# Attention and a gated two-layer network on one core: the first layer of the last four units by a Strassen scheme

## The chip, the cores and the metric

One Trainium2 chip, one of its cores. The metric is the device time of one execution in microseconds. An execution is taken several times; the median is given. A core has five engines that run side by side, each through its own list of instructions in order: PE (matrix products), DVE, ACT and POOL (elementwise work) and SP (which here only issues transfers). Semaphores tie them together.

## The reference

Attention over 4 batches, 8 heads, 768 positions and 64 dimensions, in which a query sees the keys less than 16 positions away and 24 summaries of 32 keys each; its output, 3072 tokens of 512 values, goes through a layer of 2048, a gate and a layer of 512.

```python
k_sum = k.reshape(B, H, nb, block, D).max(axis=3)
v_sum = v.reshape(B, H, nb, block, D).mean(axis=3)
scores_l = scale * np.matmul(q, k.transpose(0, 1, 3, 2))
mask_l = np.abs(pos[:, None] - pos[None, :]) < window
scores_s = scale * np.einsum('bhsd,bhnd->bhsn', q, k_sum) + np.log(block)
...
return np.matmul(a, v_all)
...
h = x @ w_in
g = np.where(h >= 1, h, np.where(h <= -1, 0.0, (h + 1) ** 2 / 4.0))
return (g @ w_out).astype(np.float32)
```

## The kernel before

The tokens are worked off in eight units of 384 (half a batch). A unit has an attention part, for four pairs of heads, and a feed-forward part. Matrix operands of the feed-forward part are split into a high half and a rest (`hi`, `lo`), and each product is the sum of three: rest by high, high by rest, high by high.

*First layer* (`ff1`, step F): for each of 16 slices f of 128 hidden values and each of four slices k of 128 inputs, three matmuls with 128 x 128 weights held in the array and 384 tokens streamed; one PSUM bank for each f, two in turn (`ps_h`). *Gate* (G, H, I, J, O): ACT takes a shifted half from PSUM and squares it, DVE takes the minimum with the value in PSUM, ACT copies the high half, POOL subtracts for the rest. *Second layer* (`ff2`, step B): for each f and each of three groups of 128 tokens, three matmuls of 512 columns into one of three PSUM banks (`ps_acc`), which collect over all f and are copied out (U) and stored (o) at the unit's end.

*Attention* (for units 2 to 7): scores for two pairs of heads at once (s), masks and maxima on DVE (n, i), exponentials on ACT (g), reciprocals on DVE (h), multiplication on POOL (l), 32 x 32 transposes on DVE (t), values on PE (p), and the split of the result into `xhi` (X, ACT) and `xlo` (L, DVE). Sums over 32 keys or values are made once for each batch (R, u, z), and copied into place by POOL (C, x).

Weights come as 64-bit numbers, and in the opening they are converted to 32 bits on ACT and DVE (a, b, c) and split by d and e; after that they stay on the chip. All transfers are issued by SP. Three texts give the order of all steps by hand, each step a letter and its indices: `OPENING`, `SECOND` and `LATER`; the last is run for each unit from 2 on. Each engine's list is the order in which the steps issue to it. PSUM has eight banks: two for F and one score block, three for `ps_acc`, three for attention.

Of the kernel before, what the change touches and what calls it, by code (L numbers as in the profile page):

```python
# [55 lines left out]
P110 H0b S13 A11 dd H0c B0a ec M130 I0b ed q21 I0c F0d0 D120 k20 ae F0d1 F0e0 F0e1 J0c F0e2 v12 F0d2 M131 J0b f130 be0
r21 f131 ce0 N120 O0c be1 E130 ce2 O0b af D130 F0d3 X11 N121 R20 ce1 F0e3 ce3 B0b L11 E131 G0d H0d I0d B0c bf1 de ee
cf1 bf0 G0e H0e T120 I0e cf0 F0f0 cf3 J0d O0d W13 F0f1 cf2 D131 F0f2 J0e df F0f3 T121 q20 G0f F110 H0f F111 W12 P121
N130 P120 N131 T130 A12 X12 I0f T131 P131 L12 F100 J0f P130 B0d O0e R21 ef O0f A13 X13 F112 L13 C20 F101 F102 F113
F103 B0e G11 G10 H10 H11 I10 B0f J10 I11 C21 F120 J11 O10 U00 F121 F122 U01 O11 F123 U02 o02 o01 o00  # L60
# [529 lines left out]
```

## Time and profile before

| | |
|---|---|
| median of 3 runs | 632.76 us (631.87 to 633.6) |
| the profiled execution | 632.96 us, of which its span is 631.2 us |
| PE busy, 272 to 344 us | 72.00 of 72.00 us |
| matmuls | 4388 on PE, as many weight loads |
| moved by DMA | 63.6 MB, all of the kernel's own by the queue of SP |

The page of the profile gives for each engine the time in which an instruction was in it. Matmuls overlap in the array, so their busy times (339 ns for one of 384 columns) are longer than the distance from one start to the next; the prediction therefore reads starts. The page divides the span into 40 slices, and shows the granted clock of the array as full from the 50th microsecond to the end.

```profile
PE   8689999999999999999999999999999999999997
DVE  5879787377836549376643737469363726411111
PEclk9879999999999999999999999999999999999999
```

### The profile page before, as it was taken

Reading aid. Unit: us, or ns where it says so; the run is one execution under the profiler, and the core shown is the slowest. Engines: PE = TensorE matmul, PEld = TensorE weight load, DVE = VectorE, ACT = ScalarE, POOL = GpSimd, SP = SyncE. Lnnn points to the kernel's source line nnn. Section 1 sums busy time; section 2 is a strip of 40 time slices with the busy share of each in tenths; the row PEclk is TensorE's granted clock in tenths of the full one; section 3 lists DMA queues with packets and bytes.
Section 4 is the critical chain, followed back from the end, with each engine's and each line's share of the span. In section 5 each row is a group of like instructions: output and inputs, shape, how many; then the busy total and the mean of one; then the engine's idle time right before and its main releaser. Section 6 shows DMA issues by size and latency. Waiting matters only on the chain.

```text
span 631.2 us, 11762 instructions
## 1 busy us (share of the span) xinstructions
PE 617.1 (98%) x4388; PEld 550.4 (87%) x4388; DVE 357.8 (57%) x822; ACT 336.7 (53%) x877; POOL 259.4 (41%) x272
## 2 busy tenths in 40 slices
PE   8689999999999999999999999999999999999997
PEld 7578888898988989898898989889898988999995
DVE  5879787377836549376643737469363726411111
ACT  2679998454547353463635436373543636343342
POOL 2578999533533333333423434333332333212221
PEclk9879999999999999999999999999999999999999
DMA  8999953181124150251213033162202210010001
GB/s 305 299 309 359 275 178 80 54 247 46 52 64 123 51 158 4 78 182 38 74 38 99 25 103 109 38 196 65 73 1 82 79 38 2 1 50 1 2 0 51
DMA packets 49770, 63.57 MB, mean 101 GB/s; under 512 B 24881, under 2 KB 33329, under 8 KB 49713
## 3 DMA queue, kind: packets, MB, share of 16 engines
q1 hardware_dynamic: 49712, 62.81, 33.5%
q8 instruction: 35, 0.57, 0.4%
q14 instruction: 23, 0.18, 0.1%
HBM read 56.51 MB, written 6.29 MB: 99 GB/s over the span
## 4 chain that ended last, share of the span: by engine, by line
PE 91%; DMA 4%; POOL 2%; DVE 1%; ACT 1%; SPq 0%; issue 0%; POOLq 0%; ACTq 0%
PE acc L464 42%; PE h L426 41%; PE o_ps L415 3%; PE s_ps L360 3%; DMA raw<-in_w_in 2%; DMA raw<-in_w_out 1%; POOL halves L175 1%; PE o_ps L332 1%; PE t_ps L320 1%; DMA first<-in_kT 1%; PE h_idle L434 0%; PE s_ps L286 0%; DVE w L163 0%; POOL e L315 0%; DVE c L158 0%
## 5 line engine op out<-in xcount | busy, mean ns | idle before, releaser
L426 PE MATMUL h<-xhi,halves 128*128 128x384 f32 x1024 | 284.7, 339 | 2.8 <-POOL halves L175 1.8
L464 PE MATMUL acc<-halves,ghi 128*128 128x512 f32 x768 | 240.4, 394 | 0.0
L455 POOL TENSOR_TENSOR glo<-t,ghi 128x384 fp32r<-128x384 f32 x128 | 129.7, 1015 | 263.7 <-ACT ghi L450 186.8
L426 PEld LDWEIGHTS h<-xhi,halves 128*128 128x128 f32 x1024 | 187.3, 188 | 9.4 <-POOL halves L175 2.7
L445 DVE SCALAR_TENSOR_TENSOR t<-h,t 128x384 f32<-128x384 f32 x128 | 70.7, 556 | 205.1 <-ACT t L442 200.4
L426 PE MATMUL h<-xlo,halves 128*128 128x384 f32 x512 | 172.0, 336 | 0.0
L464 PEld LDWEIGHTS acc<-halves,ghi 128*128 128x128 f32 x768 | 144.1, 188 | 27.8
L464 PE MATMUL acc<-halves,glo 128*128 128x512 f32 x384 | 152.4, 397 | 0.0
L439 ACT ACTIVATE t<-h,ones_half 128x384 f32<-128x384 f32 x128 | 74.0, 579 | 131.9 <-PE h L426 122.6
L405 DVE STREAM_TRANSPOSE turned_blocks<-e 32x192 f32<-32x192 f32 x288 | 106.5, 370 | 20.5 <-POOL e L393 16.4
L450 ACT CAST ghi<-t 128x384 fp32r<-128x384 f32 x128 | 65.2, 511 | 96.5 <-DVE t L445 94.8
L426 PEld LDWEIGHTS h<-xlo,halves 128*128 128x128 f32 x512 | 96.3, 188 | 4.9
L464 PEld LDWEIGHTS acc<-halves,glo 128*128 128x128 f32 x384 | 72.1, 188 | 14.5 <-issue 2.1
L381 ACT ACTIVATE e<-e,den 128x120 f32<-128x120 f32 x144 | 55.2, 386 | 26.5 <-DVE den L375 26.5
L442 ACT ACTIVATE t<-t 128x384 f32<-128x384 f32 x128 | 66.6, 522 | 2.9
L393 POOL TENSOR_TENSOR e<-e,den 128x720 f32<-128x720 f32 x24 | 33.4, 1391 | 51.0 <-DVE den L387 23.7
L175 POOL TENSOR_TENSOR halves<-w,halves 128x1024 fp32r<-128x1024 f32 x16 | 38.6, 2412 | 5.4 <-DMA q<-in_q 4.2
L381 ACT ACTIVATION_READ_ACCUMULATOR e<-e,den 128x1 f32 x144 | 27.3, 189 | 0.0
L158 DVE SCALAR_TENSOR_TENSOR c<-raw,c 128x512 int32<-128x512 int32 x32 | 22.0, 690 | 6.3 <-ACT raw L144 3.0
L368 DVE SCALAR_TENSOR_TENSOR e<-s_ps,mask_sb 128x360 f32<-128x360 f32 x48 | 22.4, 523 | 5.6 <-PE s_ps L360 5.6
L304 ACT ACTIVATE e<-e,den 128x120 f32<-128x120 f32 x48 | 18.3, 384 | 10.2 <-DVE den L299 10.2
L150 ACT ACTIVATE c<-raw 128x512 int32<-128x512 uint32 x32 | 19.8, 627 | 5.8 <-DMA raw<-in_w_in 4.8
(77 smaller groups left out, 422.3 us busy)
## 6 DMA issues: line engine op xcount, KB each, us to landing
k<-in_kwin SPq DMA_DIRECT2D x28, 360.0 KB, 4.4
v<-in_vwin SPq DMA_DIRECT2D x30, 288.0 KB, 3.4
raw<-in_w_in SPq DMA_DIRECT2D x16, 512.0 KB, 10.1
raw<-in_w_out SPq DMA_DIRECT2D x16, 512.0 KB, 10.1
out<-o SPq DMA_DIRECT2D x24, 256.0 KB, 2.3
q<-in_q SPq DMA_DIRECT2D x56, 96.0 KB, 4.0
kraw<-in_kT SPq DMA_DIRECT2D x13, 384.0 KB, 4.2
vraw<-in_vT SPq DMA_DIRECT2D x13, 384.0 KB, 5.3
```

Of the source, the lines that this page charges most:

```text
L175: nc.gpsimd.tensor_tensor(out=lo, in0=converting[i].bitcast(F32), in1=hi.bitcast(F32), op=ALU.subtract)
L368: nc.vector.scalar_tensor_tensor(out=es[c, h][:, b, j], in0=s_pss[c, p, j][:, :NT * KA].rearrange("p (t n) -> p t n", n=KA), scalar=1.0 / ...
L381: nc.scalar.activation(out=e, in_=e, func=AF.Exp, bias=dens[c, p][:, 0, j, t:t + 1], scale=1.0, accum_out=dens[c, p][:, 1, j, t:t + 1])
L393: nc.gpsimd.tensor_tensor(out=e, in0=e, in1=den.unsqueeze(2).broadcast_to([P, 2 * NT, KA]), op=ALU.mult)
L405: nc.vector.transpose(out=pt[kb * SB:(kb + 1) * SB, :, qb * SB:(qb + 1) * SB], in_=e[qb * SB:(qb + 1) * SB, :, at:at + SB])
L426: nc.tensor.matmul(hs[c, f][:, :T], weight["win", f][w][:, k * P:(k + 1) * P], x, start=(k == 0 and n == 0), stop=(k == NK - 1 and n == 2))
L439: nc.scalar.activation(out=ts[c, f], in_=hs[c, f][:, :T], func=AF.Relu, bias=ones_half, scale=0.5)
L442: nc.scalar.square(out=ts[c, f], in_=ts[c, f])
L445: nc.vector.scalar_tensor_tensor(out=ts[c, f], in0=hs[c, f][:, :T], scalar=1.0, in1=ts[c, f], op0=ALU.max, op1=ALU.min)
L450: nc.scalar.copy(out=hi, in_=ts[c, f])
L455: nc.gpsimd.tensor_tensor(out=lo, in0=ts[c, f], in1=hi.bitcast(F32), op=ALU.subtract)
L464: nc.tensor.matmul(acc[c][i], a[:, rows], weight["wout", f][w], start=(f == 0 and n == 0), stop=(f == NF - 1 and n == 2))
```

## The change

The tokens are divided anew: units of 384, 384, 256 and four of 512. From unit 3 on (`CLASSIC = 3`) the first layer is done two slices of hidden values at a time (a pair q, eight in all) by Strassen's scheme in Winograd's form. For a pair the layer is a product of two 2 x 2 block matrices: weights in blocks of 256 inputs by 128 hidden values, tokens in blocks of 256 inputs by 256 tokens. Instead of eight block products it takes seven (step 1, operands and weights being sums and differences of blocks), each of two slices of inputs by the same three split products, with 256 tokens streamed. DVE and one copy on ACT then add up the seven (step 9), through four running sums (`so_far`) and in place in PSUM. The gate works on halves of 256 tokens, and copies the high half and makes the rest for 512 at a time.

The seven weight operands of each pair are three of the old ones and four sums. These are made once, in units 1 and 2 (step %: additions on POOL and DVE, split on ACT and POOL), stored to DRAM by SP (&, six stores a pair, 48 in all), and read back in each of the four units (step {, four transfers a pair, 128 in all), issued by POOL, into a ring in the room of first-layer weights that are no longer needed. The token operands are made once for each unit: four differences on POOL (^), seven copies of high halves on ACT (<), seven subtractions on POOL (>), into the room of weights 0 to 6, one buffer each.

The second layer is issued for one group of 128 tokens at a time (step "(") and has four banks; two banks remain for attention, shared with three of the products. Scores and values are done for one pair of heads at a time. Conversions d and e of the opening are split into two instructions each, since each weight has a room of its own, and the opening no longer loads keys and queries of unit 2. One text `REST` gives the order of all steps after the opening. The core of the diff:

```diff
+BLOCKS = [[(0, 0, 6)], [(0, 6, 6)], [(1, 0, 4)], [(1, 4, 8)], [(2, 0, 8)], [(2, 8, 4), (3, 0, 4)], [(3, 4, 8)]]
+CLASSIC = 3
-SECOND = """
...
-LATER = """
...
+REST = """
+%000 r20 k20 %001 q20 %002 %010 %011 %003 %004 %012 R20 %013 %005 %006 C200 %014 s20 n200 n201 &40 r21 k21 i20 g200
...
     def convert_rest(i):
-        hi, lo = halves[i][:, 0], halves[i][:, 1]
-        nc.gpsimd.tensor_tensor(out=lo, in0=converting[i].bitcast(F32), in1=hi.bitcast(F32), op=ALU.subtract)
+        for part, piece in enumerate(pairs[i]):
+            hi, lo = weight[piece][:, 0], weight[piece][:, 1]
+            nc.gpsimd.tensor_tensor(out=lo, in0=converting[i][:, part].bitcast(F32), in1=hi.bitcast(F32), op=ALU.subtract)
...
+    def difference(c, n):
+        a, b = x_raw_tile(c, 0), x_raw_tile(c, 1)
+        out_, in0, in1 = ((a[:, 2], a[:, 1], a[:, 0]), (a[:, 1], b[:, 1], a[:, 1]), (b[:, 2], b[:, 1], a[:, 2]), (b[:, 0], b[:, 0], b[:, 2]))[n]
+        nc.gpsimd.tensor_tensor(out=out_, in0=in0, in1=in1, op=ALU.subtract)
+    def x_high(c, n):
+        x_ops[c, n] = wpool.tile([P, 2, 2, HALF], F32R, tag=f"win{n}", name=f"xop{c}_{n}")
+        nc.scalar.copy(out=x_ops[c, n][:, 0], in_=x_source(c, n))
+    def x_rest(c, n):
+        x = x_ops[c, n]
+        nc.gpsimd.tensor_tensor(out=x[:, 1], in0=x_source(c, n), in1=x[:, 0].bitcast(F32), op=ALU.subtract)
...
+    def load_set(c, q, n):
+        tag = 7 + 4 * (q % 2) + n
+        cols = sets[q, :, n * 4 * HALF:min(n * 4 + 4, 14) * HALF]
...
+        nc.gpsimd.dma_start(out=flat, in_=cols)
+    def product(c, q, n):
...
+        where, tag = ((ps_att, "att") if n in (1, 4, 5) else (ps_h, "h"))
+        hs[c, q, n] = where.tile([P, 512], F32, tag=tag, name=f"h{c}_{q}_{n}")
+        x = x_ops[c, n]
+        for kk in range(2):
+            for m, (wp, xp) in enumerate(((1, 0), (0, 1), (0, 0))):
+                nc.tensor.matmul(hs[c, q, n][:, :HALF], weights[:, wp, kk], x[:, xp, kk],
+                                 start=(kk == 0 and m == 0), stop=(kk == 1 and m == 2))
+    def combine(c, q, n):
...
+        if n == 0:
+            nc.scalar.copy(out=so_far[:, 0], in_=hs[c, q, 0][:, :HALF])
+            return
+        which, so, to = ((2, 0, 1), (4, 1, 2), (1, 0, None), (3, 1, 3), (3, 2, None), (5, 2, None), (6, 3, None))[n - 1]
+        of = hs[c, q, which][:, :HALF]
+        nc.vector.tensor_tensor(out=of if to is None else so_far[:, to], in0=of, in1=so_far[:, so], op=ALU.add)
+    def prepare(q, kk, n):
...
+            nc.gpsimd.tensor_tensor(out=a[:, 2 * n:2 * n + 2], in0=both[:, 0].bitcast(F32), in1=both[:, 1].bitcast(F32), op=ALU.add)
+        elif n < 6:
...
+            nc.vector.tensor_tensor(out=a[:, out_], in0=a[:, in0], in1=a[:, in1], op=op)
...
+                nc.gpsimd.tensor_tensor(out=a.bitcast(F32R), in0=a, in1=hi.bitcast(F32), op=ALU.subtract)
-        ps_acc = ctx.enter_context(tc.tile_pool(name="ps_acc", bufs=NTT, space=PSUM))
-        ps_att = ctx.enter_context(tc.tile_pool(name="ps_att", bufs=3, space=PSUM))
+        ps_acc = ctx.enter_context(tc.tile_pool(name="ps_acc", bufs=4, space=PSUM))
+        ps_att = ctx.enter_context(tc.tile_pool(name="ps_att", bufs=2, space=PSUM))
```

The order on PE, before, in the middle of unit 4: one slice of the first layer, then one of the second (h is the PSUM bank of a slice, acc that of 128 tokens; the last figures are the columns).

```order
L426 MATMUL h_5_4142<-xhi_2_3834,halves_727 128x384
L426 MATMUL h_5_4142<-xlo_2_3835,halves_727 128x384
L426 MATMUL h_5_4142<-xhi_2_3834,halves_727 128x384
L426 MATMUL h_5_4142<-xhi_3_3848,halves_727 128x384
L426 MATMUL h_5_4142<-xlo_3_3849,halves_727 128x384
L426 MATMUL h_5_4142<-xhi_3_3848,halves_727 128x384
L464 MATMUL acc_0_4030<-halves_727,glo_3_4113 128x512
L464 MATMUL acc_0_4030<-halves_727,ghi_3_4112 128x512 x2
L464 MATMUL acc_1_4031<-halves_727,glo_3_4113 128x512
L464 MATMUL acc_1_4031<-halves_727,ghi_3_4112 128x512 x2
```

The order on PE now, in the middle of a Strassen unit (h_4_0 is product 0 of pair 4; xop_0 its tokens, ring_4_0 its weights).

```order
L598 MATMUL h_4_0_5316<-xop_0_4500,ring_4_0_5221 128x256 x6
L598 MATMUL h_4_2_5336<-xop_2_4582,ring_4_1_5167 128x256 x6
L598 MATMUL h_4_3_5343<-xop_3_4609,ring_4_3_5241 128x256 x6
L598 MATMUL h_4_1_5358<-xop_1_4574,ring_4_0_5221 128x256 x6
L598 MATMUL h_4_4_5365<-xop_4_4624,ring_4_2_5257 128x256 x6
L694 MATMUL acc_1_4929<-halveswout_1073,glo_7_5331 128x512
L694 MATMUL acc_1_4929<-halveswout_1073,ghi_7_5330 128x512 x2
L694 MATMUL acc_0_4981<-halveswout_1073,glo_7_5331 128x512
L694 MATMUL acc_0_4981<-halveswout_1073,ghi_7_5330 128x512 x2
L598 MATMUL h_4_6_5381<-xop_6_4723,ring_4_2_5257 128x256 x6
```

A slice's twelve matmuls of 384 have become products of six matmuls of 256, and accumulations of single groups stand between them.

The order on POOL at a change of unit, before (from unit 4 to 5: rests of the gate glo, the copy of sums into keys, a multiplication of exponentials e).

```order
L455 TENSOR_TENSOR glo_15_4666<-t_15_4660,ghi_15_4665 128x384
L455 TENSOR_TENSOR glo_0_4728<-t_0_4710,ghi_0_4727 128x384
L393 TENSOR_TENSOR e_0_4725<-e_0_4725,den_0_4741 128x720
L455 TENSOR_TENSOR glo_1_4802<-t_1_4771,ghi_1_4801 128x384
L455 TENSOR_TENSOR glo_2_4855<-t_2_4820,ghi_2_4854 128x384
```

The order on POOL now, at the change from unit 2 to 3, the first with Strassen products (DMA ring is the issue of a load of weights; L486 is a difference of tokens, L498 the rest of an operand).

```order
L585 DMA ring_0_1_3321<-sets 128x1024
L585 DMA ring_1_0_3323<-sets 128x1024
L681 TENSOR_TENSOR glo_15_3311<-t_15_3244,ghi_15_3310 128x256
L629 TENSOR_TENSOR merged_1_3120<-merged_1_3120,x_1_1770 128x512
L681 TENSOR_TENSOR glo_14_3358<-t_14_3319,ghi_14_3357 128x256
L486 TENSOR_TENSOR xraw_0_2807<-xraw_1_3091,xraw_0_2807 128x512
L486 TENSOR_TENSOR xraw_1_3091<-xraw_1_3091,xraw_0_2807 128x512
L498 TENSOR_TENSOR xop_1_3361<-xraw_1_3091,xop_1_3361 128x512
L498 TENSOR_TENSOR xop_2_3386<-xraw_1_3091,xop_2_3386 128x512
L498 TENSOR_TENSOR xop_4_3407<-xraw_0_2807,xop_4_3407 128x512
L486 TENSOR_TENSOR xraw_1_3091<-xraw_1_3091 128x512
L498 TENSOR_TENSOR xop_6_3364<-xraw_1_3091,xop_6_3364 128x512
```

Where one subtraction a slice stood, there are now eight subtractions in a row, behind loads of weights and a split of weight sums.

The order on DVE before, in unit 4 (t is the gate's tile).

```order
L445 SCALAR_TENSOR_TENSOR t_11_4476<-h_11_4442,t_11_4476 128x384
L405 STREAM_TRANSPOSE turned_blocks<-e_1_4330 32x6x32 x10
L252 TENSOR_REDUCE sums<-vraw_0_4393 128x24
L253 TENSOR_SCALAR sums<-sums 128x24
L445 SCALAR_TENSOR_TENSOR t_12_4519<-h_12_4487,t_12_4519 128x384
```

The order on DVE now, in a Strassen unit (L611 adds a product to a running sum, or a running sum to a product in PSUM).

```order
L611 TENSOR_TENSOR sums_so_far<-h_4_2_5336,sums_so_far 128x256
L552 STREAM_TRANSPOSE turned_blocks<-e_2_5195 32x8x32 x3
L611 TENSOR_TENSOR sums_so_far<-h_4_4_5365,sums_so_far 128x256
L552 STREAM_TRANSPOSE turned_blocks<-e_2_5195 32x8x32 x4
L611 TENSOR_TENSOR sums_so_far<-h_4_3_5343,sums_so_far 128x256
L611 TENSOR_TENSOR h_4_1_5358<-h_4_1_5358,sums_so_far 128x256
L611 TENSOR_TENSOR h_4_6_5381<-h_4_6_5381,sums_so_far 128x256
L611 TENSOR_TENSOR h_4_3_5343<-h_4_3_5343,sums_so_far 128x256
L671 SCALAR_TENSOR_TENSOR t_8_5415<-h_4_1_5358,t_8_5415 128x256
L671 SCALAR_TENSOR_TENSOR t_9_5433<-h_4_3_5343,t_9_5433 128x256
```

Between two gate minima DVE now has seven additions for each pair of slices, each of which releases a product's bank or the gate on it.

More of the change, by code (lines that the diff above doesn't have):

```diff
@@ L56 @@
[L56 to L60, printed above, removed]
@@ L227, in window_keys @@
+        at = 0
+        for b, blk, n in BLOCKS[c]:
+            while n:
+                half, i = divmod(blk, NB)
+                m = min(n, NB - i)
+                nc.sync.dma_start(out=v_ts[c, p][:KW, at:at + m], in_=vwin[b, p, half, :, i:i + m])
+                at, blk, n = at + m, blk + m, n - m
     def window_keys(c, p):
@@ L230, in window_keys @@
         eng = {"v": nc.vector, "g": nc.gpsimd}[K_COPY[p]]
[L231 removed]
+        blocks = raws["k", c, p].rearrange("p (n q) -> p n q", q=QB)
         eng.memset(k_t[:, 0, :WIN], 0.0)
@@ new lines, in values_of_pair @@
+    def values_of_pair(c, p):
+        nt = WIDTH[c] // P
+        o_pss[c, p] = ps_att.tile([P, 512], F32, tag="att", name=f"o_ps{c}_{p}")
+        for blk in range(2 * nt):
+            t, i = divmod(blk, 2)
+            for j in range(2):
+                nc.tensor.matmul(o_pss[c, p][j * D:(j + 1) * D, blk * QB:(blk + 1) * QB], v_ts[c, p][:, blk, j * D:(j + 1) * D],
+                                 turned_blocks[:, j * nt + t, i * QB:(i + 1) * QB], start=True, stop=True)
+    hs, ts, gs, acc, outs, ring_of, merged = {}, {}, {}, {}, {}, {}, {}
@@ L457, in ff2 @@
     def ff2(c, f):
-        if f == 0:
-            acc[c] = [(ps if c == 0 else ps_acc).tile([P, DM], F32, tag="ps", name=f"acc{c}_{i}") for i in range(NTT)]
-        g_hi, g_lo = gs[c, f]
-        for i in range(NTT):
-            rows = slice(i * P, (i + 1) * P)
-            for n, (a, w) in enumerate(((g_lo, 0), (g_hi, 1), (g_hi, 0))):
-                nc.tensor.matmul(acc[c][i], a[:, rows], weight["wout", f][w], start=(f == 0 and n == 0),
-                                 stop=(f == NF - 1 and n == 2))
+        for i in range(WIDTH[c] // P):
+            ff2_rows(c, f, i)
@@ new lines, in ff2_rows @@
+    def ff2_rows(c, f, i):
+        if (c, i) not in acc:
+            acc[c, i] = (ps if c == 0 else ps_acc).tile([P, DM], F32, tag="ps", name=f"acc{c}_{i}")
+        g_hi, g_lo = gs[c, f]
+        rows = slice(i * P, (i + 1) * P)
+        first, last = (0, NF - 1) if c < CLASSIC else (1, NF - 2)
+        for n, (a, part) in enumerate(((g_lo, 0), (g_hi, 1), (g_hi, 0))):
+            nc.tensor.matmul(acc[c, i], a[:, rows], weight["wout", f][:, part], start=(f == first and n == 0), stop=(f == last and n == 2))
@@ L488, in fused_kernel @@
+        rows = mask.shape[1] * KA
+        for at, first, count in ((2, 0, 3),) if n == 0 else ((0, 2, 2), (5, 2, 2)):
+            both = bass.AP(mask.tensor, mask.offset + first * KA, [[QB * rows + KA, 2], [rows, QB], [1, count * KA]])
+            nc.sync.dma_start(out=mask_sb[:, at:at + count], in_=both)
     steps = {
```

488 lines of the change are left out of this document (318 added, 170 removed).

## The prediction

> **What bounds the kernel now.** I read the head of the page first, then the chain, then equal stretches of the steady part.
>
> ```profile
> span 631.2 us, 11762 instructions
> PE 617.1 (98%) x4388; PEld 550.4 (87%) x4388; DVE 357.8 (57%) x822; ACT 336.7 (53%) x877; POOL 259.4 (41%) x272
> PE 91%; DMA 4%; POOL 2%; DVE 1%; ACT 1%; SPq 0%; issue 0%; POOLq 0%; ACTq 0%
> core 0: us, PE busy (x) PEld busy (x) DVE busy (x) ACT busy (x) POOL busy (x), PEclk, DMA share, GB/s
> 75.00:100.00 25.00, 25.00 (x207) 21.83 (x206) 20.70 (x45) 24.54 (x62) 23.61 (x19) 1.00 0.71 187
> 272.00:344.00 72.00, 72.00 (x521) 64.37 (x521) 42.39 (x99) 35.13 (x98) 26.11 (x28) 1.00 0.28 81
> ```
>
> 91% of the chain is PE. In 272 to 344 us, one old unit, PE never rests, while DVE works 42 of 72 us, ACT 35, POOL 26. So a second of PE saved is a second gained, as long as the others keep up.
>
> Busy times overlap, so a matmul's price is its pitch, start to start:
>
> ```profile
> start us, us, engine line op out<-in xcount [idle before <-releaser]
> 614.72 0.34 PE L426 MATMUL h<-xlo,halves 128*128 128x384 f32 x1
> 614.89 0.52 PE L426 MATMUL h<-xhi,halves 128*128 128x384 f32 x2
> 615.25 0.33 PE L426 MATMUL h<-xlo,halves 128*128 128x384 f32 x1
> 615.42 0.51 PE L426 MATMUL h<-xhi,halves 128*128 128x384 f32 x2
> 615.77 0.33 PE L426 MATMUL h<-xlo,halves 128*128 128x384 f32 x1
> 615.94 0.33 PE L426 MATMUL h<-xhi,halves 128*128 128x384 f32 x1
> 616.11 0.39 PE L464 MATMUL acc<-halves,glo 128*128 128x512 f32 x1
> ...
> 618.19 0.33 PE L426 MATMUL h<-xhi,halves 128*128 128x384 f32 x1
> 9.48 3.84 PE L434 MATMUL h_idle<-zeros 128*128 128x128 f32 x32
> 78.89 0.84 PE L286 MATMUL s_ps<-k,q 64*64 64x120 f32 x24
> 79.67 0.50 PE L464 MATMUL acc<-halves,glo 128*128 128x512 f32 x1
> 299.81 1.46 PE L360 MATMUL s_ps<-k,q 64*64 64x120 f32 x48
> 301.20 0.50 PE L464 MATMUL acc<-halves,glo 128*128 128x512 f32 x1
> ```
>
> Eight matmuls of 384 columns take 616.11-614.72=1.39 us, **174 ns** each; nine of 512 take 2.08, **231 ns**. Both are 0.453 ns a column with nothing left over, so 256 columns should take **116 ns**.
>
> **The first layer.** Before: 1024+512 matmuls (rows below) by 0.174 = 267.3 us. After: units 0 and 1 keep 192 each of 384 columns (66.8 us); unit 2 has 192 of 256; each of the last four units 8 pairs x 7 products x 6 = 336 of 256. That is 1536 of 256, 178.2 us. Together 245.0: **22.3 us less**. The second layer has as many 512-column matmuls as before (768+384).
>
> The doubt is the weight load: per 256 columns as many weights are loaded as per 384 before.
>
> ```profile
> L426 PE MATMUL h<-xhi,halves 128*128 128x384 f32 x1024 | 284.7, 339 | 2.8 <-POOL halves L175 1.8
> L426 PE MATMUL h<-xlo,halves 128*128 128x384 f32 x512 | 172.0, 336 | 0.0
> L464 PE MATMUL acc<-halves,ghi 128*128 128x512 f32 x768 | 240.4, 394 | 0.0
> L464 PE MATMUL acc<-halves,glo 128*128 128x512 f32 x384 | 152.4, 397 | 0.0
> L426 PEld LDWEIGHTS h<-xhi,halves 128*128 128x128 f32 x1024 | 187.3, 188 | 9.4 <-POOL halves L175 2.7
> L455 POOL TENSOR_TENSOR glo<-t,ghi 128x384 fp32r<-128x384 f32 x128 | 129.7, 1015 | 263.7 <-ACT ghi L450 186.8
> L175 POOL TENSOR_TENSOR halves<-w,halves 128x1024 fp32r<-128x1024 f32 x16 | 38.6, 2412 | 5.4 <-DMA q<-in_q 4.2
> L393 POOL TENSOR_TENSOR e<-e,den 128x720 f32<-128x720 f32 x24 | 33.4, 1391 | 51.0 <-DVE den L387 23.7
> L262 POOL COPY v<-means 32x768 f32<-32x768 f32 x24 | 19.7, 823 | 1.5
> L445 DVE SCALAR_TENSOR_TENSOR t<-h,t 128x384 f32<-128x384 f32 x128 | 70.7, 556 | 205.1 <-ACT t L442 200.4
> L470 DVE COPY o<-acc 128x512 f32<-128x512 f32 x8 | 5.5, 683 | 4.7 <-PE acc L464 4.7
> L405 DVE STREAM_TRANSPOSE turned_blocks<-e 32x192 f32<-32x192 f32 x288 | 106.5, 370 | 20.5 <-POOL e L393 16.4
> L439 ACT ACTIVATE t<-h,ones_half 128x384 f32<-128x384 f32 x128 | 74.0, 579 | 131.9 <-PE h L426 122.6
> L381 ACT ACTIVATE e<-e,den 128x120 f32<-128x120 f32 x144 | 55.2, 386 | 26.5 <-DVE den L375 26.5
> L381 ACT ACTIVATION_READ_ACCUMULATOR e<-e,den 128x1 f32 x144 | 27.3, 189 | 0.0
> L450 ACT CAST ghi<-t 128x384 fp32r<-128x384 f32 x128 | 65.2, 511 | 96.5 <-DVE t L445 94.8
> L144 ACT ACTIVATE raw<-raw 128x1024 f32<-128x1024 f32 x16 | 18.3, 1144 | 0.0
> q1 hardware_dynamic: 49712, 62.81, 33.5%
> 626.70 1.29 SPq L476 DMA_DIRECT2D out<-o  x3
> ```
>
> A load shows 188 ns busy, but loads overlap: the 32 idle products, each with its own load of 128 columns, start (3.84-0.27)/31=115 ns apart (0.27 being about one product's own time), although they stream only 128 columns. So loads flow at 115 ns or better, and the pitch at 256 lies between 115 and, were the loads' busy time the limit, 188. I take 116, the value two rows give. There is no reserve: each ns more costs 1536 ns, and at 116+22.3/1.536=131 ns the gain is gone.
>
> The Trainium skill, "TensorE: Matmul & The Clock Gate", section on LDWEIGHTS, has a load take its columns divided by 1.2 per ns, here 107 ns by that rule. By that rule the load stays under the 116 ns and the sum stands; the trace's 115 ns agree nearly, and no run here shows the load against 256 columns.
>
> **Attention on PE.** As many small products as before, in more blocks. A block of 24 lasts 79.67-78.89=0.78 us to the next accumulation, one of 48 1.39: 25 ns each and 0.17 at a block's entry. After unit 1 the old kernel has 24 blocks of 48, the new one 32 of 32 and 8 of 16: 16 more entries, **+3 us** (0 to 5).
>
> **The other engines in a Strassen unit.** PE: 336 x 0.116 + 192 x 0.231 + eight blocks of (0.17+32 x 0.025=0.97) = 39.0+44.4+7.8 = **91 us**.
> DVE, by 1.0 ns an element (L445 to L470: 127 ns for 128 elements): an operation of 256 on PSUM 0.43. 56 combinations (seven a pair) 24.1, 32 gate minima 13.8, 48 transposes of 256 (370 ns at 192, so some 0.44) 21.0, masks, maxima, reciprocals and copies of 512-token shapes some 14 by the same scaling: **73 us**, and 12 more in the units (3 and 4) in which the next batches' keys and values are summed. That is 80 to 93% of PE; before it was 42 of 72.
> ACT, by 0.83 ns an element (L450 to L144: 633 ns for 640): 32 half gates and 32 squares of 256 at 0.47 or less, 30.1; 16 casts of 512 at 0.62, 9.9; 32 exponentials of 0.386+0.189, 18.4; some 19 copies, 10: 68 us, no bound.
> POOL: a subtraction costs 0.18+2.18 ns an element (1015 ns at 384, 2412 at 1024): 1.30 us at 512. 16 gate rests and 11 for the x operands: 35.1; eight norms of 480 elements (by L393, 0.99) 7.9; copies (L262) 6: **49 us, plus 32 issues of ring loads**.
>
> What an issue on POOL costs the old trace cannot show: its only kernel queue is q1, issued by SP. Below: nothing. Nearest row: SP's three issues in 1.29 us, 0.43 each. Above: 2.3 us, the landing time of a 256 KB store on the page (out<-o, last figure of its row below). I take 0.43, so POOL has 49+14=63 us; both ends stay in the range.
>
> ```profile
> out<-o SPq DMA_DIRECT2D x24, 256.0 KB, 2.3
> ```
>
> The Trainium skill, "DMA: Bandwidth & Descriptors", section on latency, gives about 1 us to the first byte for a DMA issued from GpSimd, because software writes its descriptors. By that figure as an estimate POOL has 49+32=81 us, still under PE's, and the sum would be unchanged but tighter; no run here shows it yet.
>
> Where DVE runs at 80 to 93% behind a PE that takes its products in a fixed order, some combinations come late. Four PSUM banks serve the seven products and attention. I take 1 us a unit, **+4 us** (0 to 20).
>
> **The change to Strassen.** Unit 3's last pair of heads leaves PSUM just before its products. Behind it POOL has ^31, ^32, >31, >32, >34, ^33, >36, >35 in a row: 8 x 1.30=10.4, with the copy (0.68) before them 11.1 us until the product of operand 5 may start. PE has ahead of that one the scores (0.97), four groups of accumulation (0.69 each) and six products (0.70): 7.9. It waits 3.2 there, and 1 more for glo_1, which POOL makes behind two norms and a copy: **+4.5 us** (2 to 12, since POOL comes there behind weight sums and eight issues). At the three later changes of unit the subtractions lie among a dozen accumulations, which hide them; without that cover it would be some 4 us each.
>
> **The tail.** After the last product PE has four groups (2.8 us) until glo_15 is ready: two combinations of 0.43, two half gates and two squares of 0.47, minimum 0.43, cast 0.62, rest 1.3, on three engines in turn some 5. **+2 us** (1 to 4).
>
> **The opening.** Each conversion of 1024 becomes two of 512: on POOL 2 x 1.30-2.41=0.19 sixteen times; on ACT 2 x 0.72-1.14=0.30 for each of L144's sixteen. ACT and POOL are near full in 75 to 100 us, but PE is full too, on weights already converted; four sums and the loads of the next batch also leave the opening. **+1 us** (0 to 6).
> The weight sums (32 additions of 256 at 0.74 and 16 subtractions of 512, 44 us on POOL) lie in units 1 and 2 beside 26 us of rests, 13 of norms and 10 of copies: 93 of the some 116 us that PE has there (27 and 22 of the first layer, 33 and 22 of the second, 12 of attention). Hidden, except in the 4.5 above. The loads move 1.84 MB a pair, 160 GB/s over 11.4 us of PE, beside DMA engines that are 0.28 busy at 81 GB/s (row of 272 to 344 us): some 0.8, nothing on the path; if they came late, each product would wait for its load's landing.
>
> **Sum:** -22.3+3+4+4.5+2+1 = -7.8. The profiled execution took 632.96 us (span 631.2), 0.2 over the median of 632.76, so I take it as it is: **625.2 us**.
>
> **Rivals.**
> 1. *POOL becomes the bound by issuing.* From the first product to the end POOL has 64 rests (83 us), the operands of four units (57), 24 norms (24) and copies (18), 182 us without issues; PE has four times 83.4 without attention, attention of three units and a rest of unit 2 and 3, some 363. 123 of the 128 issues lie in that stretch, so it decides from (363-182)/123=1.5 us an issue. At 1.9 us POOL needs 416, 53 more than PE; without any waits the sum is 617, so **670 us**, slower. For it: nothing is known between 0.43 and 2.3, and POOL works in order, so that a ring load that waits for PE holds the rests behind it. Against: the nearest row. 0.14.
> 2. *The weight load sets the pitch.* From 131 ns slower; at 188 ns 1536 x 0.072=111 us, **736 us**. Against: 115 ns in the idle products. 0.05; for 120 to 131 ns, 631 to 648, 0.08.
> 3. *DVE's lateness eats the gain*: 93% full in units 3 and 4; 3 to 5 us a unit, 12 to 20 in all, **633 to 641 us**. 0.14.
> 4. *The order hides all*: no waits but tail and blocks, **612 to 618 us**. 0.15.
> My forecast, 619 to 630: 0.44.
>
> Faster by over 0.3% (1.9 us, what a measurement tells from no change): the forecast, the fourth rival and a quarter of 120 to 131 ns, 0.61; within 0.3%: parts of the second and third, 0.09; slower 0.30. The range leaves out the first rival and the 188 ns, 0.19: 612 to 650; the forecast's own is 619 to 630.
>
> **What will show it.** Pitch of the new product line: 116 ns. Sums by stretch in a Strassen unit: PE near 91 of some 92 us, DVE 73 to 85, POOL 63. A gap of about 4 us ahead of product (3,0,5). An issue of ring loads on POOL: 0.43 us, and gate rests not waiting behind it. Wrong if the pitch is over 120, POOL's issues take over 1.5 us, or PE's waits for DVE pass 5 us a unit.

## The result, and the profile after

The changed kernel takes **661.62 us** (658.13 to 664.29) beside 633.16 for the kernel before in the same runs: 1.045 times as long, with an interval of 1.040 to 1.050. Forecast were 625.2 us and a range of 612 to 650. The profiled execution took 661.37 us, its span 659.6: 28.4 us more than before, where the sum said 7.8 less. So **36 us** have to be explained.

First the page of the changed kernel: its head, the row of PE, the clock, the software queue and the chain.

```profile
span 659.6 us, 13521 instructions
PE 618.7 (94%) x4772; PEld 538.7 (82%) x4772; DVE 466.3 (71%) x1081; ACT 375.8 (57%) x1042; POOL 428.2 (65%) x515
PEclk8989999989999999899999999999989999998999
q0 software_dynamic: 18432, 58.73, 29.0%
PE 63%; DVE 11%; DMA 11%; ACT 6%; POOL 4%; issue 4%; SPq 0%; DVEq 0%; ACTq 0%; POOLq 0%
```

No engine has become the bound: POOL is busy 65%, DVE 71%. But PE's share of the chain fell from 91 to 63%, and the clock row has an 8 here and there to the end, where before it was 9 from the fourth slice on.

The next rows are the windows view, one row a unit (from the first matmul of a unit's first layer to that of the next; the last ends with PE's last matmul), units 1 to 6. The columns are start and end, length, busy time of PE, weight loads, DVE, ACT, POOL, granted clock, DMA share and GB/s.

```profile
111.10:197.30 86.20, 78.62 (x545) 67.19 (x544) 64.63 (x164) 41.17 (x103) 54.79 (x68) 0.96 0.64 194
197.30:256.10 58.80, 56.50 (x495) 48.31 (x493) 51.79 (x106) 37.42 (x120) 45.85 (x57) 1.00 0.75 224
256.10:362.00 105.90, 99.39 (x843) 85.87 (x844) 86.95 (x206) 59.67 (x180) 75.77 (x90) 0.98 0.85 251
362.00:455.70 93.70, 92.67 (x776) 81.56 (x775) 74.74 (x178) 53.81 (x163) 63.87 (x80) 1.00 0.77 229
455.70:556.10 100.40, 98.26 (x768) 86.53 (x767) 68.00 (x160) 55.46 (x156) 65.38 (x75) 0.98 0.62 186
556.10:654.40 98.30, 92.52 (x553) 81.92 (x551) 35.19 (x90) 40.33 (x95) 40.56 (x47) 0.98 0.42 134
```

Unit 4 (fourth row) takes nearly what was forecast: 93.7 us against 92, POOL 63.9 against 63. DVE's 74.7 us are those of a unit without the sums of keys and values (73), though the forecast put 12 more into this unit; ACT's 53.8 are 14 below the 68 of the forecast. The other units lose. PE is idle 7.6 us in unit 1, 2.3 in unit 2, 6.5 in unit 3, 1.0, 2.1 and 5.8 in units 4 to 6 (length less busy): **25 us**, where the old units 1 to 6 had none. And the clock is below full in four of the six.

What ended those waits, by the view of PE's waits (total, times, longest), with the rows of the page for the new work:

```profile
PE s_ps L512 <- POOL k L359: 5.9, 1, 5.9
PE h L598 <- DMA ring<-sets: 4.8, 4, 2.4
L585 POOL DMA_DIRECT2D ring<-sets x128 | 70.7, 558 | 36.0 <-PE h L598 31.0
L623 DVE TENSOR_TENSOR merged<-merged 128x128 f32<-128x128 f32 x64 | 33.2, 528 | 7.0 <-POOL merged L620 5.6
ring<-sets POOLq DMA_DIRECT2D x96, 512.0 KB, 5.6
out<-o SPq DMA_DIRECT2D x24, 256.0 KB, 5.3
```

An issue on POOL costs 0.558 us (0.43 was taken), a ring load lands after 5.6 us, and a result's store now lands after 5.3 us where it was 2.3. POOL stood 31.0 us at ring loads whose buffers PE still read (second number of the L585 row's end).

### The profile page after: what moved, and what is told of

Read it like the earlier page. It is cut to its first block, busy times and chain, and to the rows that moved or that the text cites. A ratio compares the mean times of both kernels' runs of the same rounds, so it can differ in the third digit from the quotient of the medians.

```text
span 659.6 us, 13521 instructions
## 1 busy us (share of the span) xinstructions
PE 618.7 (94%) x4772; PEld 538.7 (82%) x4772; DVE 466.3 (71%) x1081; ACT 375.8 (57%) x1042; POOL 428.2 (65%) x515
## 4 chain that ended last, share of the span: by engine, by line
PE 63%; DVE 11%; DMA 11%; ACT 6%; POOL 4%; issue 4%; SPq 0%; DVEq 0%; ACTq 0%; POOLq 0%
PE acc L694 30%; PE h L598 20%; PE h L573 6%; DMA ring<-sets 3%; DVE merged L623 3%; DMA kraw<-in_kT 3%; DMA out<-o 3%; PE s_ps L512 2%; PE o_ps L561 2%; DMA k<-in_kwin 2%; DVE t L671 1%; DVE turned_blocks L552 1%; ACT e L423 1%; POOL glo L681 1%; DMA vraw<-in_vT 1%
## 5 line engine op out<-in xcount | busy, mean ns | idle before, releaser
L694 PE MATMUL acc<-halveswout,ghi 128*128 128x512 f32 x768 | 239.7, 393 | 0.0
L681 POOL TENSOR_TENSOR glo<-t,ghi 128x512 fp32r<-128x512 f32 (+2 forms) x112 | 126.8, 1135 | 115.1 <-ACT ghi L676 102.4
L598 PEld LDWEIGHTS h<-xop,ring 128*128 128x128 f32 x1344 | 176.7, 192 | 25.7 <-DVE t L671 6.5
L598 PE MATMUL h<-xop,ring 128*128 128x256 f32 x1344 | 184.1, 286 | 11.8 <-DMA ring<-sets 4.8
L694 PEld LDWEIGHTS acc<-halveswout,ghi 128*128 128x128 f32 x768 | 145.6, 190 | 25.8
L694 PE MATMUL acc<-halveswout,glo 128*128 128x512 f32 x384 | 154.1, 401 | 2.7 <-ACT o L705 1.7
L663 ACT ACTIVATE t<-h,ones_half 128x256 f32<-128x256 f32 (+1 forms) x176 | 84.2, 489 | 100.7 <-DVE h L611 76.7
L573 PE MATMUL h<-x,halveswin 128*128 128x384 f32 (+1 forms) x576 | 104.8, 329 | 4.7 <-DVE t L671 3.0
L552 DVE STREAM_TRANSPOSE turned_blocks<-e 32x256 f32<-32x256 f32 (+1 forms) x240 | 98.3, 409 | 7.0 <-POOL e L540 3.1
L573 PEld LDWEIGHTS h<-x,halveswin 128*128 128x128 f32 x576 | 91.9, 191 | 13.5 <-DVE t L671 5.1
L585 POOL DMA_DIRECT2D ring<-sets x128 | 70.7, 558 | 36.0 <-PE h L598 31.0
L611 DVE TENSOR_TENSOR h<-h,sums_so_far 128x256 f32<-128x256 f32 x128 | 52.2, 427 | 31.9 <-PE h L598 31.1
L611 DVE TENSOR_TENSOR sums_so_far<-h,sums_so_far 128x256 f32<-128x256 f32 x96 | 39.7, 420 | 41.3 <-PE h L598 38.2
L623 DVE TENSOR_TENSOR merged<-merged 128x128 f32<-128x128 f32 x64 | 33.2, 528 | 7.0 <-POOL merged L620 5.6
L498 POOL TENSOR_TENSOR xop<-xraw,xop 128x512 fp32r<-128x512 f32 x28 | 36.1, 1300 | 1.8 <-ACT xop L494 1.6
## 6 DMA issues: line engine op xcount, KB each, us to landing
rawwin<-in_w_in SPq DMA_DIRECT2D x16, 512.0 KB, 10.5
```

The costliest lines, as they stand in the source:

```text
L552: nc.vector.transpose(out=turned_blocks[kb * SB:(kb + 1) * SB, :2 * nt, qb * SB:(qb + 1) * SB], in_=e[qb * SB:(qb + 1) * SB, :, at:at + SB])
L573: nc.tensor.matmul(hs[c, f][:, :w], weight["win", f][:, part, k * P:(k + 1) * P], x, start=(k == 0 and n == 0), stop=(k == NK - 1 and n == 2))
L585: nc.gpsimd.dma_start(out=flat, in_=cols)
L598: nc.tensor.matmul(hs[c, q, n][:, :HALF], weights[:, wp, kk], x[:, xp, kk], start=(kk == 0 and m == 0), stop=(kk == 1 and m == 2))
L611: nc.vector.tensor_tensor(out=of if to is None else so_far[:, to], in0=of, in1=so_far[:, so], op=ALU.add)
L663: nc.scalar.activation(out=t, in_=h, func=AF.Relu, bias=ones_half, scale=0.5)
```

## The experiments

Eighteen runs. All but the thirteenth were timed beside the kernel before on the same chip, whose medians lay between 632.0 and 633.0 us.

| run | median us | ratio to before, interval |
|---|---|---|
| 1 late scores | 670.55 | 1.060 (1.055 to 1.064) |
| 2 no weight sums | 657.91 | 1.041 (1.035 to 1.047) |
| 3 no reloads of the ring | 644.96 | 1.019 (1.018 to 1.021) |
| 4 no combinations | 658.08 | 1.042 (1.038 to 1.046) |
| 5 early loads | 662.33 | 1.047 (1.045 to 1.050) |
| 6 ring loads on SP | 662.79 | 1.049 (1.046 to 1.052) |
| 7 results' own tiles | 661.62 | 1.046 (1.042 to 1.050) |
| 8 plain products of 512 | 727.71 | 1.151 (1.147 to 1.154) |
| 9 = 2 + 3 + 4 | 637.43 | 1.008 (1.006 to 1.010) |
| 10 keys first (with 5) | 659.43 | 1.042 (1.034 to 1.050) |
| 11 on SP from unit 4 | 652.56 | 1.033 (1.030 to 1.035) |
| 12 = 10 + 11 + 7 | 650.35 | 1.029 (1.026 to 1.033) |
| 13 narrow products (one execution) | 659.47 | |
| 14 = 10 + 2 | 652.29 | 1.032 (1.026 to 1.037) |
| 15 = 12, a key sum later | 650.57 | 1.029 (1.022 to 1.036) |
| 16 = 9 + 10 | 633.24 | 1.0005 (0.9993 to 1.0017) |
| 17 = 12, the right sum later | 654.42 | 1.035 (1.033 to 1.037) |
| 18 = 10 + 11 + 17's move | 657.84 | 1.041 (1.039 to 1.043) |

Differences from the changed kernel are given by medians. The runs were on three chips; by the ratios to the kernel before the differences come out up to 2 us smaller. The changed kernel's own four executions lie up to 6 us apart.

### What the side work costs: runs 2, 3, 4 and 9

Run 2 drops all steps `%` from the order, and `keep` stores other weights. Run 4 drops all steps `9`. Run 3:

```diff
 def load_set(c, q, n):
+    if (c, q) not in ((CLASSIC, 0), (CLASSIC, 1)):
+        ring_of[c, q][n] = ring_of[CLASSIC, q % 2][n]
+        return
```

> Left out: the 128 operations that add and subtract weights (48 on POOL, 64 on DVE, 16 on ACT); the stores to the DRAM buffer stay in number, size and place, with other contents. Theory (the sums are not hidden): unit 2 took 58.8 us where two thirds of an old unit are 49.1, and unit 3's first 12 us start among leftovers of it; 8 to 14 us less, 648 to 654. Rival (sums hidden as predicted, the excess is the DMA traffic): 0 to 4 us less.

> Left out: 120 of the 128 ring loads; the first two sets stay in the ring and serve all pairs. Theory (DMA contention and POOL's queue): PE's waits for ring loads (4.8 us), for result tiles whose store takes 5.3 us, and the low clock after them go in units 3 to 6; 8 to 15 us less, 647 to 654. Rival (the waits there come from the order of DVE's and ACT's work): only the 4.8 us of ring waits or less, 0 to 5 us less.

> Left out: the 224 additions on DVE and 32 copies on ACT that combine the products; the gates read the products' banks. Theory (DVE at 80% follows well enough: unit 4 ran with PE busy 92.7 of 93.7 us): 3 to 8 us less, 653 to 659, mostly at the start of unit 3. Rival (the third one of the prediction, DVE's lateness eats the gain everywhere): 15 us less or more, 646 or below.

> Left out together: the weight sums, 120 of 128 ring loads and the combinations (each alone gave 3.7, 16.7 and 3.5 us). Theory (many late hand-offs, each held by more than one thing, so that taking one away uncovers the next): together more than the 24 us of the parts, 628 to 636, with what is left in unit 1 and at the start of unit 3. Rival (they are separate losses): their sum, 637 to 641. Second rival (they hide one another's gain and the order itself costs): 642 or more.

Measured by medians: the sums are worth 3.7 us, the reloads **16.7**, the combinations 3.5; together 24.2. Only the reloads are clear of the noise: the intervals of runs 2 and 4 overlap that of the change. Run 9's total is its first rival's (separate losses, 637 to 641), and the parts add up to 23.9. By the ratios they are 2.4, 16.3 and 1.7, together 20.4 against 23.3 in run 9, and the intervals leave some 8 us of play. So the losses may be separate, but that they add is not shown closer than that. For run 2 the size fits the rival (0 to 4 us), for run 3 the theory (a little above it), for run 4 the theory, though no gain at all is not excluded there. In run 3 the last unit runs without a gap, 89.9 us in place of 98.3, with DMA at 0.04 in place of 0.42; result stores land there after 2.8 us, where the change has 5.3. Unit 2 of run 2 loses its idle time, 55.6 us in place of 58.8. First the last unit and the stores of run 3, then unit 2 of run 2:

```profile
548.10:638.00 89.90, 89.90 (x553) 80.62 (x551) 34.95 (x90) 40.51 (x95) 26.94 (x21) 1.00 0.04 15
out<-o SPq DMA_DIRECT2D x24, 256.0 KB, 2.8
```

```profile
197.10:252.70 55.60, 55.46 (x494) 48.47 (x492) 36.89 (x78) 32.73 (x111) 28.66 (x37) 1.00 0.77 227
```

### The start of unit 2: runs 1, 5, 10, 14 and 16

The longest wait, 5.9 us, begins at 127.1 us, PE's first scores of unit 2. The chain of waits of the changed kernel there (start, length, what):

```profile
125.52 0.98 ACT o L705 x2
126.52 0.35 SPq L709
...
128.02 3.38 DMA kraw<-in_kT
131.42 0.95 DVE ks L354
132.40 5.72 DMA vraw<-in_vT
138.14 0.96 DVE sums L369
...
147.09 0.56 DVE t L671
```

The raw keys were loaded in the opening before. Now their load stands behind unit 0's three stores on SP, which wait for ACT's copies. Then DVE must sum them, and the raw values, and the gates stand behind both.

Run 1 puts the scores behind more products; run 5 puts the loads first again (keys and queries of unit 2 in tiles that unit 1 has left); run 10 also puts the key sum and its copy (R20, C200) ahead of the weight sums; run 14 is run 10 without weight sums, run 16 is run 9 with run 10.

```diff
 run 1: -... s20 n200 n201 ... i20 g200 ... F130 F131 ... F142
        +... F130 F131 ... F142 s20 n200 n201 i20 g200
 run 5: OPENING  -A12 X12 ... ef O0f A13 X13 F112 L13
                 +A12 r20 X12 ... ef k20 O0f A13 r21 X13 q20 F112 L13 k21
 run 10: OPENING -J10 I11 F120
                 +J10 I11 R20 C200 F120
```

> Same work; the scores of unit 2's first pair of heads, their masks, maxima and exponentials stand some 6 us of TensorE work later in every engine's order. Theory (a load moved behind the stores): unit 2's first raw keys now stand on SP behind unit 0's three stores, and the scores wait 6.2 us at 126.7 us for them, after which the clock is granted at half for 6.8 us. With other products ahead the wait is covered: 5 to 8 us less, 653 to 657. Rival (the helpers are late there as a whole, so the wait turns up at the next product): 0 to 3 us less.

> Same work; five loads of unit 2 (two tiles of raw keys, two of windowed keys, one of queries) are issued in the opening again, ahead of unit 0's three stores, into buffers that unit 1 has left. Theory (the loads are late, and the late DVE sum of keys holds the gates behind it in DVE's order, so that in the first experiment PE waited 8.5 us for a gate in place of 6.3 for the scores): the wait at 126.7 us goes, and the stretch of half clock behind it; unit 1 falls from 86.2 to 80 to 82 us, 654 to 658 in all. Rival (the DMA engines are full there, and the loads land as late as before): 0 to 2 us less.

> Same work; the early loads of the fifth run, and the sum of unit 2's first keys (DVE) and its copy (POOL) stand ahead of the weight sums. Theory (two things held the first scores of unit 2, the load behind the stores on SP and the key sum behind the weight sums on DVE; each alone leaves the wait): the 5 to 6 us wait at 127 to 133 us and the half clock behind it go, unit 1 falls from 86 to 77 to 80 us, 653 to 656 in all. Rival (a third thing holds them, or the time is lost again in unit 2): 659 or more.

> The tenth run with the weight sums left out. Theory (in the tenth run the scores of unit 2 came in time, but DVE then worked without a break from 130.5 to 145 us, seven to nine of its operations weight sums, and PE waited 3.8 us for a gate instead): unit 1 falls from 82.8 to 77 to 80 us, unit 2 by 3; 646 to 652 in all. Rival (the key and value sums and the turned blocks alone fill DVE there): unit 1 at 82 or more, 655 or more.

> The ninth run (no weight sums, no reloads, no combinations) with the changes of the tenth. Theory (what was left over the kernel before is the wait in unit 1 and the pitch): 6 to 9 us less than the ninth's 637.4, 628 to 631. Rival (the order costs it elsewhere too): 634 or more.

Runs 1 and 5 were misses. In run 1 the wait came back as 7.9 us for a gate, behind two key sums and a value sum in DVE's list, each of which waited for its load, and the kernel got slower. In run 5, whose total is its rival's, the load was in time, but the key sum stood behind weight sums, and nothing was gained. Run 10 brought 2 us, not the 6 to 8 of its theory (its rival's 659), and its interval holds the changed kernel's ratio. Its chain shows why: the scores came in time, and the burst of work on DVE was still there, first the weight sums (below), then masks, two more sums and turned blocks:

```profile
129.05 1.41 POOL merged L621 x2
130.49 0.82 DVE merged L624
```

Run 14 ended inside neither forecast for its unit: unit 1 fell from 82.8 to 81.4 us, so the weight sums are only a part of what fills DVE. Its total is 7.1 us below run 10's, mostly by units 2 and 3, which is more than the 3.7 of run 2. Run 16 is 4.2 us faster than run 9, so unit 1's start costs about that in a kernel without the side work. It takes **633.24 us, as long as the kernel before**, which lies between its theory (628 to 631) and its rival (634 or more). What PE does in it, units 1, 3 and 4:

```profile
112.00:191.90 79.90, 75.74 (x545) 65.07 (x543) 49.72 (x129) 36.51 (x96) 29.99 (x40) 1.00 0.71 216
247.60:348.00 100.40, 96.88 (x845) 84.88 (x844) 66.96 (x150) 56.90 (x173) 58.51 (x60) 1.00 0.46 132
348.00:440.00 92.00, 92.00 (x776) 81.74 (x775) 52.95 (x122) 51.40 (x153) 47.11 (x47) 1.00 0.25 71
```

4.2 us of idle PE are left in unit 1 and 3.5 in unit 3, none in unit 4. So even without weight sums, reloads and combinations, the rest of the change (units, order, token operands, more attention blocks) gives back all that the shorter first layer saves.

### Where the ring loads are issued: runs 6 and 11

```diff
-nc.gpsimd.dma_start(out=flat, in_=cols)
+nc.sync.dma_start(out=flat.bitcast(F32), in_=cols)      # run 6 in all units, run 11 from unit 4 on
```

> Same work; the 128 ring loads are issued by SP in place of POOL. Theory (issuing on POOL costs 71 us there and holds gate rests while a load waits for its buffer, and POOL's other work holds loads): units 3 to 6 get 4 to 10 us shorter, 651 to 657. Rival 1 (the loads are late because the transfers are slow): no change within 2 us. Rival 2 (on SP a load that waits for PE now holds the key and value loads behind it): slower by 3 us or more.

> Same work; ring loads of unit 3 on POOL, those of units 4 to 6 on SP. Theory (sixth run: with all on SP, unit 6 took 90.0 us in place of 97.9 and unit 5 the same, while unit 3 took 9 us more because its loads stood behind SP's waits at the change): the gain without the loss, 7 to 10 us less, 651 to 655. Rival (the loads of unit 6 only came early because everything before was later): 0 to 3 us less.

Run 6's total fits its first rival (no change), but not its reason: unit 6 gained (98.3 to 90.3 us) and unit 3 lost (105.9 to 114.7). Run 11 keeps the gain without the loss: 9.1 us less than the change, unit 6 at 90.4 us and PE busy through it. The transfers are the same. They stand in another list, and the issue costs less there: 0.38 us in the median on SP, where POOL's 0.56 us each also take POOL's time. These two were not tested apart. First POOL's list in the changed kernel, then SP's in run 11, for the same loads:

```profile
585.49 0.53 POOL L585 DMA_DIRECT2D ring<-sets  x1 [2.64 <-PE h L598]
588.47 1.60 POOL L585 DMA_DIRECT2D ring<-sets  x3 [2.45 <-issue]
```

```profile
582.17 1.74 SPq L588 DMA_DIRECT2D ring<-sets  x4
555.10:645.50 90.40, 90.32 (x553) 80.65 (x551) 35.02 (x90) 40.39 (x95) 26.91 (x21) 1.00 0.40 137
```

All four have left by 583.9 us in run 11 and by 590.1 in the changed kernel, while unit 6 began only 1 us apart (555.1 and 556.1). On POOL they stand among gate rests that wait for ACT and PE.

### A late load behind DVE's name: runs 7, 12, 15, 17 and 18

> Same work; the four result tiles of each of units 3 to 6 lie in buffers of their own (the operand tiles' second buffers) in place of the two that they shared. Theory (a result copy waits for an earlier store, 5.3 us to landing, and PE for the bank: 1.7 us of PE's waits, 13.6 of DVE's, 7.6 of ACT's, and gates queue behind those copies): 3 to 6 us less, 655 to 658. Rival (these waits lie off the path): 0 to 2 us less.

> Same work; the last two together, and result tiles of their own. Theory (separate losses in separate units, so they add): 640 to 648. Rival (the time is lost again in the next unit): 653 or more.

> The twelfth run with one operation moved: the sum of unit 4's fourth keys (DVE) stands some ten operations later. Theory (its load took 9.9 us to land, DVE waited for it with the gate minima behind it, and PE waited 4.5 us 'for DVE'): that wait goes, with the half clock behind it, unit 3 falls from 109.6 to 103 to 106 us, 645 to 648 in all. Rival (the wait was DVE's own lateness): 650 as before.

> The twelfth run with one operation moved. The fifteenth run moved the sum of unit 4's fourth keys, but the sum for which DVE waited (4.3 to 4.8 us) is that of unit 5's first keys, whose load is issued six steps ahead of it; now that one stands some 30 DVE operations later, just ahead of the copy that needs it. Theory (a late load holds DVE's queue and with it the gates): PE's wait of 4.5 us at 336 us goes, unit 3 falls from 109.6 to 103 to 106 us, 645 to 648 in all. Rival (DVE itself is late there): 650 as before.

> The same without the result tiles of their own (the seventh run gave nothing): what the changes that helped give together, all work done. Theory (they add): unit 1 as in the tenth, 4 to 6 as in the eleventh run, 642 to 647. Rival (lost again): 650 or more. Neither theory takes it below the kernel before.

```diff
 run 7: -o_sb = att.tile([P, DM], F32, tag="merged", ...)
        +o_sb = xpool.tile([P, 3, DM], F32, tag=f"x{i // 2}", ...)[:, i % 2]    # c >= CLASSIC
 run 15: R43 behind 9326;  runs 17 and 18: R50 ahead of C501, 56 steps later
```

Run 7: nothing, as its rival said; PE's wait for a result copy went, and its waits for ring loads grew from 4.8 to 7.5 us. Run 12 gave 650.35, between its two theories. In its profiled execution, the slowest of the four (653.82 us), unit 3 took 109.6 us, 3.7 more than in the change. PE's longest wait there is 3.7 us and is put down to DVE, though DVE itself waited 4.7 us, here by its timeline and the chain (the expectations of runs 15 and 17 give PE's wait as 4.5 us):

```profile
325.17 9.90 DMA kraw<-in_kT
335.17 0.95 DVE L355 TENSOR_REDUCE ks<-kraw 128x24 f32<-128x768 f32 x1 [4.70 <-DMA kraw<-in_kT]
336.04 0.41 DVE L675 SCALAR_TENSOR_TENSOR t<-h,t 128x256 f32<-128x256 f32 x1
```

The key load that DVE waits for here, 9.9 us, took 7.8 us to land in the changed kernel and 3.9 in run 3. Run 15 moved another sum than the one that waits, and tells nothing on it. Run 17 moved the right one: the wait that ended at 336 us went, as its theory said, but no time was gained (by medians 4 us were lost, on another chip, and the intervals touch). It came back a dozen microseconds later as waits for ring loads:

```profile
341.06 0.87 DVE ks L355
...
343.44 8.00 DMA ring<-sets
...
351.57 4.44 PE h L602 x23
```

Run 18 was to be the best of all and missed: 657.84. It differs from run 17 only in the result tiles, which run 7 had found worth nothing, and here they are worth 3.4 us. So the gains place by place don't add where the transfers stay; in run 17 the next late load took the time. The fastest versions with all work done are runs 12 and 15, 650 us. No version here beats the kernel before.

### The pitch: run 13

```diff
+cols = HALF if kk == 0 and m == 0 else 192
-nc.tensor.matmul(hs[c, q, n][:, :HALF], ..., x[:, xp, kk], ...)
+nc.tensor.matmul(hs[c, q, n][:, :cols], ..., x[:, xp, kk, :cols], ...)
```

> Left out: in five of the six matmuls of each product the last 64 of 256 columns. Looked at for the pitch alone. If the stream of columns sets it (0.453 ns a column), the six take 120 + 5 x 88 = 560 ns; if the weight load does, at the 112 to 115 ns that the idle products of 128 columns show, 120 + 5 x 113 = 685 ns; if the load's floor is the 120 ns itself, 720 as before.

Thirty products in a row, first the changed kernel, then run 13, each up to the start of the next accumulation:

```profile
292.06 3.74 PE L598 MATMUL h<-xop,ring 128*128 128x256 f32 x30
295.63 0.40 PE L694 MATMUL acc<-halveswout,glo 128*128 128x512 f32 x1
```

```profile
291.72 3.56 PE L599 MATMUL h<-xop,ring 128*128 128x256 f32 x30
295.11 0.46 PE L695 MATMUL acc<-halveswout,glo 128*128 128x512 f32 x1
```

(295.63-292.06)/30 = **119 ns** at 256 columns. With 25 of the 30 cut to 192 it is 113 ns a matmul, 678 for six: the 685 of the second case, not 560. So the 25 narrow ones take (30 x 113 - 5 x 119)/25 = 112 ns, near the 115 of the idle products with 128 columns: between 128 and 192 columns the pitch hardly depends on them, and 256 columns lie 7 ns above. That this floor is the weight load was not tested apart from other fixed costs. Over all of run 16 the median pitch of the 256-column matmuls is 120 ns.

### Plain products of 512: run 8

> Units and order of loads as in the change, but the first layer of units 3 to 6 by plain products of 512 columns (384 of them a unit; the rest of x is written and the head read in its place); weight sums, ring, operands and combinations left out. Without any waits its units take what four thirds of an old unit do, 98.1 us, against 92.6 of Strassen. Theory (the re-division of units is harmless after unit 2, the side work of Strassen costs the time): 632 to 642, so that in place of 22 us gained, 20 to 30 are lost to the side work. Rival (the larger units and the moved loads themselves bring most of the excess): 650 or more.

This run doesn't decide between theory and rival, although its total lies in the rival's range. Its order was derived step for step from the change's, and has waits of its own; by the view of PE's waits 24 us for the gate's rest on POOL. It says nothing on units of 512 as such.

```profile
PE acc L661 <- POOL glo L648: 24.0, 14, 3.6
```

## Why the prediction was wrong

| term | forecast us | by the runs us |
|---|---|---|
| first layer | -22.3 | -17.7 (119 in place of 116 ns, 1536 times) |
| ring loads | 0 | +16.7 (run 3) |
| combinations | +4 | +3.5 (run 4, not clear of the noise) |
| weight sums | 0 but in the transition | +3.7 (run 2, not clear of the noise) |
| start of unit 2 | 0 | +4.2 (run 16 against 9) |
| all else: blocks, transition, tail, opening | +10.5 | +18.0 (what is left in run 16: 0.3 over before, and the 17.7) |
| sum | -7.8 | +28.4 |

The right column comes to the 28.5 measured because its sixth row is a remainder. The split rests on runs 2, 3 and 4 adding up to run 9, which is shown to some 8 us.

What the remainder holds can be read from run 16's trace, start to start over every matmul, beside the trace of the kernel before. The first layer takes 260.5 us where it took 274.0, so 13.5 less and not 17.7; scores and values take 53.0 where they took 49.5; PE is idle 22.4 us between matmuls and at the end where it was 13.1. That is 4.2, 3.5 and 9.3 of the 18.0; the other 1.0 is spread.

**The step that failed** is "some 0.8, nothing on the path", on the ring loads. It compared 160 GB/s with the room left on the DMA engines, and took a load that lands within its pair as free. The share itself was right: 0.77 to 0.85 in units 3 and 4. But the transfers weren't free. Its own next clause, that a late load would cost its landing, was the better guide. Run 3 prices the reloads at 16.7 us, and the runs show three ways: products wait for ring loads (4.8 us); issuing on POOL costs its time and puts the loads among gate rests (run 11: 9.1 us less); and other transfers take longer, result stores 5.3 us against 2.8 without reloads, and one key load 7.8 against 3.9, with DVE's gates behind it. How the 16.7 divides among the three is not shown.

The Trainium skill, "DMA: Bandwidth & Descriptors", section on the anatomy of one DMA, fits a transfer from GpSimd as 2.0 us and its bytes by 436 GB/s, which for 512 KB is an estimate of 3.2 us. This trace's median is 5.6: by that fit a load would be 2.4 us sooner than it is beside the other transfers of this kernel (251 GB/s in unit 3), and the measured landing decides.

**Weight sums "hidden, except in the 4.5".** The sum counted POOL's operations and forgot DVE's: 64 additions at 528 ns, 33 us, which made DVE 51.8 us busy in unit 2's 58.8. The error is 3.7 us by run 2 and 7.1 by run 14 against run 10.

**The move past SP's queue** was left at +1 for the opening: that unit 2's first loads now stand behind three stores was not asked, nor what DVE has queued behind the key sum. Run 16 shows 4.2 us there, run 1 that DVE's sums and their loads, not the scores alone, were the thing waited for.

**The pitch** was right in kind: 119 ns for 116, no column law broken. The size was off by 4.6 us (6.1 by run 16's median of 120), on the side that the prediction had said it had no reserve on.

**DVE's lateness**, +4: 3.5 measured, within the noise. POOL's issues, rival 1: 0.558 us, not the bound, as taken; but that rival's other argument, that a ring load that waits for PE holds the rests behind it, came true (31.0 us of POOL's waits), and the forecast gave it no price. The work of each engine in unit 4: PE and POOL right to 2 us, DVE 10 and ACT 14 us below the forecast, which cost nothing as neither is the bound. The blocks of attention, +3, were right (3.5 in run 16). The gap of about 4 us ahead of product (3,0,5) did not appear: PE waited 0.69 us there, and 5.2 us in seven short waits from 255 to 281 us, so the +4.5 was near the sum for another reason than the row of subtractions. The signs that were to show a mistake (a pitch over 120, issues over 1.5 us, over 5 us of waits for DVE a unit) stayed silent while the forecast was 36 us off, because each priced one engine's work, and the time went into waits between engines and transfers.

**Open** stays what causes the idle time in the sixth row. Some 7.7 us of it lie in units 1 and 3 of run 16, and unit 0 has 4.0 where it had 2.3; no run takes these waits away, and how much of any wait is the clock behind it was not separated.

## What to carry to other kernels

A kernel with PE at 100% has no slack for its helpers: when the change takes 3% of PE's work, price the transfers that it adds by every other load's landing time, and by every list in which they stand, not by bandwidth alone. When a wait is named, walk back through the list of the engine that is named to the first instruction that waited itself; moving the consumer, or one of two causes, moves the wait. And test whether losses add before naming one cause.
